# Gate and value products of two token chunks as a 2x2 block multiplication with seven products

## The chip, the cores and the metric

The kernel runs on one core of a Trainium2 chip. The metric is the time of one execution in device microseconds (us). The engines of the core are called as in the profile: PE (TensorE, matrix products), DVE (VectorE), ACT (ScalarE), POOL (GpSimd) and SP (SyncE, which issues the DMAs). Products are collected in PSUM, which has eight banks of 128 x 512 fp32; everything else lies in SBUF.

## What is computed

Attention with a mask by clusters, a first MLP with a squared ReLU, and a second MLP with a gate. The change concerns the second MLP:

```python
def _moe2_ref(x, w_gate, w_val, w_out):      # x: 1536 x 512
    gate = 1.0 / (1.0 + np.exp(-(x @ w_gate)))   # w_gate, w_val: 512 x 1536
    val = x @ w_val
    return (gate * val @ w_out).astype(np.float32)   # w_out: 1536 x 512

x = _moe_ref(x=attention, **moe_kwargs)      # relu(x @ w_in) ** 2 @ w_out
return _moe2_ref(x=x, **moe2_kwargs)
```

`w_gate` is drawn 200 times as large as the other matrices, and all is fp32.

## The kernel before

**Tiling.** The 1536 tokens are three chunks of 512 (`NCH`, numbers 0, 1, 2), the model width 512 is four tiles of 128 (`KD`), and the width 1536 of the second MLP is twelve tiles of 128 (`NF2`, index f). Tensors are kept transposed: the output y of the first MLP is, for each chunk, four tiles of 128 x 512 (feature x token), and a gate or value product of one chunk and one f is one PSUM bank of 128 x 512.

**Precision.** An fp32 factor is scaled by a power of two and split into two f16 tiles, a high part (`copy`, L368, most often on ACT) and a low part, the rest (`rest`, L1634, a SCALAR_TENSOR_TENSOR on DVE). A product of two such pairs is three matmuls: high x high, high x low, low x high. So the gate product of one (chunk, f) is 4 tiles x 3 = 12 matmuls into a bank `pg`, the value product 12 into a bank `pv` (`g3_half`); over 3 chunks and 12 f's that is 864 matmuls.

**Weights.** For each f, SP loads a raw tile `wgr` and one `wvr` (128 x 512). They are then brought to a form that can be split exactly: the magnitude on ACT (L1487), a clamp on POOL (L1495, in place), a shift and two bit operations on DVE (L1502, L1509, L1516), giving `wgm` and `wvm`. ACT takes their largest sum (L353), PE adds over partitions (bank `sm`), DVE makes the power of two (L612 to L622, tiles of 128 x 2), and the split gives the pairs `wgp` and `wvp`. The twelve `w2` tiles, for the last product, go the same way.

**A gate and value step.** When `pg` of (chunk, f) is full, ACT takes a tanh out of it (L1926, tile `th`), which frees the bank; when `pv` is full, DVE makes `gv` = (th + 1) * pv (L1933), which frees that one. ACT then bounds `gv` (L2157), PE and DVE turn the bounds of eight or four f's into powers of two (`gm`, L1769 to L1990), and `gv` is split into `gs` (ACT high, DVE low) for the last product `o`, which has 432 matmuls. U (L2138) is the small product of two powers of two that the tanh and the bound need. `yf` (L1903) adds up parts of y on DVE as their banks come.

**What sets the order.** PE's order of products is the list `order`: the first MLP of chunk 0, then of chunks 1 and 2, then the gate and value steps (`g3`), for f = 0 and 1 chunk by chunk, from f = 2 on all three chunks for each f, then `o` (`g4`). The order of every other instruction on every engine is worked out when the kernel is built, by a list scheduler (`Planner`) that has a priority and a price on each engine for each task; the table `PLAN` holds priorities and tie-breakers. An engine runs its instructions in that order, each waiting for its inputs and for its buffers: PSUM banks are handed out from pools of 1, 2, 4 and 1 banks, big tiles from a pool of slabs.

Of the kernel before, what the change touches and what calls it, by code (L numbers as in the profile page):

```python
# [33 lines left out]
    "c_hi_v": 5490, "clamp_p": -17626, "conv": 25, "conv_gate": 10, "d": -72.6, "dup_a": 10516,  # L34
    "dup_p": -33301, "dup_q": 32564, "e_bufs": 2, "exp": 0.0, "fill_less": 250, "fill_most": 12,
    "fill_step": 215, "g_gate": 121, "g_most": 14.9, "g_split": -3.9, "group": 4, "h_gate": 16,
    "h_split": -8.5, "hi": 30.7, "hi_a": -33311, "hi_p": 105282, "hip_p": 1853, "hip_v": 19873,
    "keep_x_v": -47, "kept": 1, "kept2": 0, "lead": 0, "lead2": 51, "lead_min": 9.2,
    "lead_slope": 0, "lo": -0.2, "lo_v": 18934, "load_gate": 42, "margin": 13, "max": -0.2,
    "oh_p": 86, "pe_keep": 3.3, "pe_keep_v": 15244, "pe_turn": 92.9, "pv": 2.6, "pv_pe": 65.6,  # L40
    "qk": -3.4, "qk_hi_a": -33970, "qk_hi_p": 34925, "qk_lo_v": 24610, "qk_sc_p": -14028, "raw": 27,
    "relu": -72.7, "s_hi_a": -3303, "s_hi_p": -6526, "s_lo_v": -10971, "spare": 0,
    "split_gate": 116, "square_v": 6751, "third": 1, "turn": -5.4, "v_hi_a": -4766, "v_hi_p": 15239,
    "v_later": 100000, "v_lo_v": -10993, "v_split": 4.8, "v_stat": 6.0, "w_hi_a": 4334,
    "w_hi_p": 8749, "w_lo_v": -9747, "w_load": 9.4, "w_mag_v": 20242, "w_split": 25.5,
    "wait_a": 0.19, "wait_p": 0.07, "wait_q": 0.1, "wait_t": 0, "wait_v": 0.18, "worth_a": -17439,
    "worth_p": -5542, "worth_v": 4863, "x": -1.2, "x0": 194, "x1": 67, "x_gate": 2, "x_split": 8.1,
    "y_gate": 43, "y_keep": 9.9, "y_keep_v": 30618, "y_split": 45.6,
# [162 lines left out]
def kernel(  # L211
# [13 lines left out]
    nc = tc.nc  # L225
# [384 lines left out]
    def power(src, inv, scale):  # L610
# [8 lines left out]
        nc.vector.tensor_scalar(  # L619
            out=inv, in0=inv, scalar1=float(2.0 ** -14), scalar2=None, op0=ALU.mult  # L620
        )
        nc.vector.reciprocal(out=scale, in_=inv)  # L622
# [834 lines left out]

    class Weights:
        def __init__(self, src, name, tiled, uses, whole=(), col=None, known=False):
# [4 lines left out]
            self.known = known  # L1464
            self.raw, self.m, self.parts = {}, {}, {}
            self.conv = {}
# [55 lines left out]
        def tasks(self, f, uses):  # L1522
            k = uses[0]
            pr = pr_of(k, CONV)
            t = add(
                lambda e: self.load(f), {"q": 2100}, pr - PLAN["w_load"], take=[("st", 1)],
                gate=near(k, LOADGATE),
            )

            room = (k, CONVGATE, 1)  # L1530
            t = add(
                lambda e: self.magnitude(e, f), {"a": 560, "v": 335}, pr, kind="w_mag", after=[t],
                take=[("S", 1)], gate=room,
            )
            t = add(lambda e: self.clamp(e, f), {"v": 335, "p": 600}, pr, kind="clamp", after=[t])
# [17 lines left out]
        def bound_task(self, f, k):  # L1553
            def most(e):
# [5 lines left out]
                most, {"a": 625}, pr_of(k, PLAN["w_split"]), after=[self.conv[f]], take=[("S", 1)],  # L1560
                gate=(k, SPLITGATE, 2),
            )

        def pair_tasks(self, f, k, after):
            mh = hold("S", 1, 2)
# [8 lines left out]
            def lo(e):  # L1574
# [3 lines left out]
                drop(self.m.pop(f))  # L1578

            a = add(  # L1580
                hi, {"a": 617, "v": 400, "p": 790}, pr_of(k, PLAN["w_split"]), after=after + [self.conv[f]],
                kind="w_hi", give=[mh], take=[("S", 1)] if self.known else [],
# [3 lines left out]
                lo, {"v": 664, "p": 1980}, pr_of(k, PLAN["w_split"]), after=[a], give=[mh], kind="w_lo",  # L1586
# [145 lines left out]
    xpair = {}  # L1732
    u1done = {}
# [23 lines left out]
    WG = Weights(w_gate, "wg", True, w3, col=lambda f: NF1 + 2 * f)  # L1757
    WV = Weights(w_val, "wv", True, w3, col=lambda f: NF1 + 2 * f + 1)
    wdone = {}
    for f in range(NF2):  # L1760
        wdone[f] = scale_pairs([(WG, f), (WV, f)], w3[f][0])
        for w in (WG, WV):
            w.pair_tasks(f, w3[f][0], [wdone[f]])
# [11 lines left out]
    for j, fs in enumerate(FS):  # L1775
# [9 lines left out]
        def powers(e, cs=cs, box=box):  # L1785
# [120 lines left out]
    def g3_half(e, kind, c, f, k):  # L1906
# [10 lines left out]
        if c == NCH - 1:  # L1917
            W.done(f, at_["g3", 0, f])
# [86 lines left out]

    for k, (kind, c, f) in enumerate(order):
# [39 lines left out]
        elif kind == "g2":  # L2046
# [28 lines left out]
            if tail_g:  # L2075
                k3 = at_["g3", c, 0]
# [213 lines left out]
```

## Time and profile before

| | us |
|---|---|
| median of three runs (781.5 to 783.2) | 781.68 |
| the profiled execution, its own time | 780.43 |
| its span, first to last instruction | 778.7 |
| y part of the first MLP, last stretch before the gate products | 431.7 to 494.1 |
| gate and value stage (864 matmuls `pg`, `pv`) | 494.1 to 681.5 |
| last product `o` and the end | 681.5 to 778.7 |

The profile gives each instruction's engine, line, output and inputs, start and duration. The table of stretches says how busy each engine was in each; the chain of waits follows the work that ended last back to what released it; the timeline gives one engine's instructions in order of start, where "x2" is two of a kind in a row and the second number the time from the first one's start to the last one's end. Instructions of DVE overlap a little: the next starts before the one ahead has ended, so how many fit into a stretch is read from the distance of starts, not from the durations.

### The profile page before, as it was taken

The numbers are of one execution on the slowest core, as the hardware profiler recorded it, in microseconds if no ns is written. First come the engines' busy times: TensorE is split into PE (matmuls) and PEld (weight loads), VectorE is DVE, ScalarE is ACT, GpSimd is POOL, SyncE is SP. The second block draws the span as 40 slices with busy tenths as digits, with TensorE's granted clock in tenths as the row PEclk, the third lists the DMA queues.
The fourth block names the chain that finished last, engine by engine and source line by source line (L and its number), as shares of the span: only waits on it lengthen the run. The fifth ranks groups of instructions, "written<-read, shape, count | busy, mean of one in ns | idle before, by whom it ended". The sixth has DMA issues, their size and how long they took to land.

```text
span 778.7 us, 13069 instructions
## 1 busy us (share of the span) xinstructions
PE 748.8 (96%) x4865; PEld 449.0 (58%) x4865; DVE 568.0 (73%) x1111; ACT 539.6 (69%) x1036; POOL 190.0 (24%) x240
## 2 busy tenths in 40 slices
PE   8999898799999989999999999999999999999998
PEld 5667776556565557744448888544444444444443
DVE  6899899999999998877776458964445799572012
ACT  7999899989877887699995224855555798462100
POOL 7553654444424422111222110110010021010000
PEclk9999999999999999999999999999999999999999
DMA  6767697976557787732323233322112223000012
GB/s 239 179 162 155 159 220 181 207 190 152 157 161 190 191 191 158 237 109 90 107 76 122 92 109 109 108 68 97 55 54 65 77 79 106 1 1 0 1 68 94
DMA packets 132768, 93.77 MB, mean 120 GB/s; under 512 B 114657, under 2 KB 114849, under 8 KB 132705
## 3 DMA queue, kind: packets, MB, share of 16 engines
q1 hardware_dynamic: 132704, 92.95, 43.3%
q8 instruction: 38, 0.62, 0.4%
q14 instruction: 26, 0.20, 0.1%
HBM read 60.00 MB, written 3.15 MB: 81 GB/s over the span
## 4 chain that ended last, share of the span: by engine, by line
PE 68%; DVE 14%; ACT 12%; issue 3%; DMA 2%; POOL 1%; SPq 0%; DVEq 0%; ACTq 0%
PE y L361 14%; PE pv L361 12%; PE pg L361 12%; PE o L361 12%; PE g L361 12%; DVE nm L1072 4%; ACT s L1087 3%; PE s L361 3%; ACT hl L368 3%; DVE hl L1112 3%; PE po L361 2%; DVE wo0m L1509 1%; ACT vh L368 1%; ACT e L1087 1%; DVE wo0m L1516 1%
## 5 line engine op out<-in xcount | busy, mean ns | idle before, releaser
L361 PE MATMUL pv<-y,wvp 128*128 128x512 f16 x432 | 99.3, 379 | 0.0
L361 PE MATMUL pg<-y,wgp 128*128 128x512 f16 x432 | 99.2, 379 | 0.0
L361 PE MATMUL s<-M,T 128*128 128x384 f32 x360 | 86.3, 365 | 9.7 <-DVE hl L1112 5.2
L1072 DVE TENSOR_REDUCE nm<-s 128x1 f32<-128x768 f32 x96 | 90.1, 950 | 7.3 <-PE s L361 6.7
L361 PE MATMUL o<-w2p,gs 128*128 128x512 f16 x432 | 93.5, 379 | 0.0
L361 PEld LDWEIGHTS s<-M,T 128*128 128x128 f32 x360 | 60.4, 190 | 23.2 <-DVE hl L1112 11.2
L361 PEld LDWEIGHTS <-gs 128*128 128x128 f16 x432 | 42.1, 98 | 50.6
L361 PEld LDWEIGHTS <-wgp 128*128 128x128 f16 x432 | 42.0, 98 | 50.6 <-issue 0.3
L1087 ACT ACTIVATE s<-s,nm 128x768 f32<-128x768 f32 x67 | 58.8, 877 | 16.3 <-DVE nm L1072 12.9
L361 PEld LDWEIGHTS <-wvp 128*128 128x128 f16 x432 | 41.2, 98 | 48.6
L361 PE MATMUL g<-x,wi0p 128*128 128x512 f16 x288 | 66.8, 384 | 2.0 <-DVE g_12l L1686 2.0
L1112 DVE TENSOR_TENSOR hl<-s,hl 128x768 f16<-128x768 f32 x67 | 63.6, 949 | 5.0 <-ACT hl L368 4.9
L361 PE MATMUL g<-x,wi1p 128*128 128x512 f16 x288 | 62.4, 379 | 0.0
L368 ACT ACTIVATE hl<-s 128x768 f16<-128x768 f32 x67 | 54.6, 815 | 1.1
L1966 DVE SCALAR_TENSOR_TENSOR ot<-o,G,ot 128x512 f32<-128x512 f32 x12 | 9.0, 751 | 59.6 <-PE o L361 59.6
L1933 DVE SCALAR_TENSOR_TENSOR gv<-th,pv 128x512 f32<-128x512 f32 x36 | 24.5, 683 | 38.1 <-PE pv L361 38.0
L2157 ACT ACTIVATE gs<-gv,U 128x512 f32<-128x512 f32 x36 | 25.8, 718 | 36.0 <-DVE gv L1933 36.0
L361 PEld LDWEIGHTS <-pt 128*128 128x128 f16 x1296 | 42.2, 98 | 9.4 <-issue 8.7
L361 PEld LDWEIGHTS <-wi1p 128*128 128x128 f16 x288 | 28.1, 98 | 33.8
L361 PE MATMUL po<-vh,pt 128*128 128x64 f16 x864 | 44.8, 193 | 2.5 <-DVE xp L1230 2.5
L361 PEld LDWEIGHTS <-wi0p 128*128 128x128 f16 x288 | 27.0, 99 | 34.7 <-issue 6.0
L361 PE MATMUL y<-h,wo0m 128*128 128x512 f32 x96 | 44.2, 596 | 0.8 <-DVE ptc L1185 0.8
(376 smaller groups left out, 1594.8 us busy)
## 6 DMA issues: line engine op xcount, KB each, us to landing
wi0r<-in_moe_w_in_dram SPq DMA_DIRECT2D x16, 512.0 KB, 3.9
wo0r<-in_moe_w_out_dram SPq DMA_DIRECT2D x16, 512.0 KB, 3.8
wo1r<-in_moe_w_out_dram SPq DMA_DIRECT2D x16, 512.0 KB, 3.5
wi1r<-in_moe_w_in_dram SPq DMA_DIRECT2D x12, 512.0 KB, 3.7
wgr<-in_moe_w_gate_dram SPq DMA_DIRECT2D x12, 512.0 KB, 3.3
wvr<-in_moe_w_val_dram SPq DMA_DIRECT2D x12, 512.0 KB, 4.0
w2r<-in_moe_w_out_dram SPq DMA_DIRECT2D x12, 512.0 KB, 4.2
raw<-in_q_dram SPq DMA_DIRECT2D x8, 384.0 KB, 4.1
```

The source lines that it names most:

```text
L361: nc.tensor.matmul(o, lhsT=l, rhs=r, start=a, stop=z)
L368: nc.scalar.activation(out=out, in_=in_, func=AF.Copy, scale=scale)
L1072: nc.vector.tensor_reduce(out=NM[n], in_=sc_ps[n][:, :, :HS], axis=AX.XY, op=ALU.max, negate=True)
L1087: nc.scalar.activation(out=y, in_=x, func=AF.Exp, bias=NM[n], accum_out=SM[n // NQ][:, i : i + 1],)
L1112: nc.vector.tensor_tensor(out=halves(hl[:, n % 2, 1]), in0=x[:, :, :HS], in1=halves(hl[:, n % 2, 0]), op=ALU.subtract,)
L1509: nc.vector.scalar_tensor_tensor(out=mi, in0=self.words(f)[1], scalar=-0x40000000, in1=mi, op0=ALU.bitwise_and, op1=ALU.bitwise_or,)
L1516: nc.vector.scalar_tensor_tensor(out=mi, in0=self.words(f)[0], scalar=29, in1=mi, op0=ALU.logical_shift_right, op1=ALU.bitwise_or,)
L1933: nc.vector.scalar_tensor_tensor(out=o, in0=t, scalar=1.0, in1=p, op0=ALU.add, op1=ALU.mult)
L1966: nc.vector.scalar_tensor_tensor(out=o, in0=p, scalar=by, in1=o, op0=ALU.mult, op1=ALU.add)
L2157: nc.scalar.activation(out=t.rearrange("p a k -> p (a k)").bitcast(F32), in_=gv[c, f], func=AF.Abs, scale=U3[:, c, f, 1:2], accum_out=GA[: ...
```

## The change

Chunk 0 stays as it was, 24 products of 12 matmuls. For chunks 1 and 2 two neighbouring f's are taken together: with the model width in two halves, the products of two chunks and two f's are a 2x2 matrix of blocks times another, once for the gate (`pg`) and once for the value (`pv`), so there are six pairs of f and twelve such "quads". A quad has seven block products a to g in place of eight. A block product has half the depth, 2 tiles x 3 = 6 matmuls, and a bank of its own; a quad is 42 matmuls in place of 48. What comes with it:

- Sums of weight blocks: for each pair of f's and each of `wgm`, `wvm`, four subtractions or additions of 128 x 256 into the tiles `wgs_0`, `wgs_1` (or `wvs`), 48 in all, which stand on POOL; their split gives `wgq` (or `wvq`), 24 high parts and 24 low ones.
- Sums of y blocks: eight of 128 x 512 on DVE (`yT`, L2449), after chunk 2's last `yf`, and their split. Chunks 1 and 2 now have one scale in common (`ys1`).
- A quad's results: product a is copied out of its bank by ACT (X); seven additions on DVE, each of a bank and an SBUF tile (L2224, 84 in all), join X, U, Y and Z, which become the four results.
- The tanh (L2270) and the value step (L2277) of chunks 1 and 2 then read and write SBUF tiles.
- PE's order: chunk 0 for f = 0 to 3, then in turn quad `pg` and quad `pv` of one pair and two f's of chunk 0; the last two pairs stand without chunk 0 between.
- The scale of two f's is made at once (`sm` six times with 4 columns, not twelve times with 2); the split of three `wo1` low parts stands on DVE instead of POOL. The loads are the same, in another order.

```diff
 PLAN = {
-    "c_hi_v": 5490, "clamp_p": -17626, "conv": 25, "conv_gate": 10, "d": -72.6, "dup_a": 10516,
+    "comb": 142.0, "comb_p": -23566, "comb_v": -9423, "conv": 25, "conv3": 8.1, "conv_gate": 10,
...
-    PRE = 2
-    for c in range(NCH):
-        order.extend(("g3", c, f) for f in range(PRE))
-    for f in range(PRE, NF2):
-        for c in range(NCH):
-            order.append(("g3", c, f))
+    PRE = PLAN["pre"]
+    order.extend(("g3", 0, f) for f in range(PRE))
+    for i in range(NF2 // 2):
+        order.extend((("q", "pg", i), ("q", "pv", i)))
+        order.extend(("g3", 0, f) for f in range(PRE + 2 * i, PRE + 2 * i + 2) if f < NF2)
...
+            if n == 0:
+                tt(out=x, in0=mb[:, :HD], in1=mb[:, HD:], op=ALU.add)
+                tt(out=y, in0=x, in1=ma[:, :HD], op=ALU.subtract)
+            else:
+                tt(out=x, in0=ma[:, :HD], in1=mb[:, :HD], op=ALU.subtract)
+                tt(out=y, in0=ma[:, HD:], in1=S[0][:, HD:], op=ALU.subtract)
...
+            t = add(
+                comb, {"v": 680, "p": 1400}, pr, kind="comb", after=[w.conv[a], w.conv[b]] + ([t] if t else []),
...
+        def product(nm, left, right):
+            p = Q[nm] = bank(f"{kind}{nm}{i}")
+            n = 0
+            for kk, (lh, ll) in enumerate(left):
+                rh, rl = TY[right, kk]
+                for x, y in ((lh, rh), (lh, rl), (ll, rh)):
+                    mm(p, x, y, n == 0, n == 5)
+                    n += 1
...
+                nc.vector.tensor_tensor(out=Q[out], in0=Q[one], in1=Q[other], op=ALU.add)
...
+        t = on_pe("a", lambda: cols(a, 0), "B11", prev + w1_, [wa])
...
+        t = on_pe("b", lambda: sums(1), "T2", [t] + sp[:2], [sh[0]])
+        u2 = join("U", "X", "b", t, [s1])
+        t = on_pe("c", lambda: sums(2), "T3", [t] + sp[2:], [sh[1]])
+        u3 = join("Y", "U", "c", t, [u2])
+        t = on_pe("d", lambda: sums(0), "T1", [t], [sh[0]])
+        c22 = join("Z", "Y", "d", t, [u3], free=False)
+        u4 = join("U", "U", "d", t, [c22])
+        t = on_pe("e", lambda: cols(a, 1), "B21", [t], [wa])
+        c11 = join("X", "X", "e", t, [u2])
+        t = on_pe("f", lambda: cols(b, 1), "T4", [t] + w2_, [wb])
+        c21 = join("Y", "Y", "f", t, [c22])
...
+        c12 = join("U", "U", "g", t, [u4])
...
+                o = yt[n, kk] = slab(F32, f"y{n}_{kk}")
+                eng(e).tensor_tensor(out=o, in0=src(x, kk), in1=src(y, kk), op=ALU.subtract)
```

Two engines' orders show what the planner makes of it. A row is one instruction: its line, its operation, its output tile, its inputs and its size.

DVE of the kernel before, in the middle of the gate and value stage: the low parts of one f's weights, two value steps, the conversion of the next f's weights, a value step.

```order
L1634 SCALAR_TENSOR_TENSOR wgp_2091_6777<-wgm_2079_6746,WS,wgp_2091_6777 128x512
L1634 SCALAR_TENSOR_TENSOR wvp_2093_6781<-wvm_2083_6750,WS,wvp_2093_6781 128x512
L1933 SCALAR_TENSOR_TENSOR gv_3_2108_6843<-th_3_2102_6817,pv_3_2101_6804 128x512
L1933 SCALAR_TENSOR_TENSOR gv_3_2118_6877<-th_3_2113_6860,pv_3_2112_6847 128x512
L1502 TENSOR_SCALAR wgm_2117_6875<-wgm_2117_6875 128x512
L1502 TENSOR_SCALAR wvm_2121_6879<-wvm_2121_6879 128x512
L1509 SCALAR_TENSOR_TENSOR wgm_2117_6875<-wgr_2015_6534,wgm_2117_6875 128x512
L1509 SCALAR_TENSOR_TENSOR wvm_2121_6879<-wvr_2022_6544,wvm_2121_6879 128x512
```

DVE of the changed kernel, at the second quad: a value step of chunk 0, then the seven joins of `pg`'s products b to g and the first two of `pv`'s.

```order
L2039 SCALAR_TENSOR_TENSOR gv_5_2229_7060<-th_5_2195_6976,pv_5_2190_6958 128x512
L2224 TENSOR_TENSOR pgU_2236_7074<-pgX_2201_6997,pgb_2200_6990 128x512
L2224 TENSOR_TENSOR pgY_2240_7078<-pgU_2236_7074,pgc_2204_7001 128x512
L2224 TENSOR_TENSOR pgX_2201_6997<-pgX_2201_6997,pge_2216_7032 128x512
L2224 TENSOR_TENSOR pgZ_2249_7099<-pgY_2240_7078,pgd_2209_7018 128x512
L2224 TENSOR_TENSOR pgU_2236_7074<-pgU_2236_7074,pgd_2209_7018 128x512
L2224 TENSOR_TENSOR pgY_2240_7078<-pgY_2240_7078,pgf_2223_7047 128x512
L2224 TENSOR_TENSOR pgU_2236_7074<-pgU_2236_7074,pgg_2233_7065 128x512
L2224 TENSOR_TENSOR pvU_2260_7131<-pvX_2253_7113,pvb_2250_7102 128x512
L2224 TENSOR_TENSOR pvY_2264_7141<-pvU_2260_7131,pvc_2256_7117 128x512
```

Between two pairs of weight conversions, where one value step per chunk stood, DVE now has the joins, and each of six banks of a quad is freed by one of them.

POOL of the kernel before, in the same stage: the clamps of two f's weights, and nothing between.

```order
L1495 TENSOR_SCALAR wgm_2117_6875<-wgm_2117_6875 128x512
L1495 TENSOR_SCALAR wvm_2121_6879<-wvm_2121_6879 128x512
L1495 TENSOR_SCALAR wgm_2155_7004<-wgm_2155_7004 128x512
L1495 TENSOR_SCALAR wvm_2159_7008<-wvm_2159_7008 128x512
L1495 TENSOR_SCALAR wgm_2193_7133<-wgm_2193_7133 128x512
```

POOL of the changed kernel, near the start of the stage: between the clamps stand the eight sums of one pair of f's, four for the gate (`wgs`) and four for the value (`wvs`).

```order
L1508 TENSOR_SCALAR wgm_2022_6490<-wgm_2022_6490 128x512
L1508 TENSOR_SCALAR wvm_2069_6655<-wvm_2069_6655 128x512
L1822 TENSOR_TENSOR wgs_0_2130_6796<-wgm_1934_6261 128x256
L1823 TENSOR_TENSOR wgs_0_2130_6796<-wgs_0_2130_6796,wgm_1903_6212 128x256
L1822 TENSOR_TENSOR wvs_0_2139_6814<-wvm_1978_6385 128x256
L1823 TENSOR_TENSOR wvs_0_2139_6814<-wvs_0_2139_6814,wvm_1910_6230 128x256
L1825 TENSOR_TENSOR wgs_1_2149_6835<-wgm_1903_6212,wgm_1934_6261 128x256
L1826 TENSOR_TENSOR wgs_1_2149_6835<-wgm_1903_6212,wgs_0_2130_6796 128x256
L1825 TENSOR_TENSOR wvs_1_2155_6851<-wvm_1910_6230,wvm_1978_6385 128x256
L1826 TENSOR_TENSOR wvs_1_2155_6851<-wvm_1910_6230,wvs_0_2139_6814 128x256
L1508 TENSOR_SCALAR wgm_2140_6817<-wgm_2140_6817 128x512
```

The sums stand in the queue beside the clamps of the next f's, in six such groups of eight; the first two groups stand before the last `yf` of DVE, the other four behind it.

## Rows read from the trace of the kernel before

**Rows 1.** First part of the page: busy time and share of each engine.

```profile
PE 748.8 (96%) x4865; PEld 449.0 (58%) x4865; DVE 568.0 (73%) x1111; ACT 539.6 (69%) x1036; POOL 190.0 (24%) x240
```

**Rows 2.** Table of stretches: from:to, length, busy of each engine (instructions), granted clock, DMA.

```profile
431.70:494.10 62.40, 62.40 (x278) 51.42 (x276) 40.72 (x86) 22.41 (x49) 9.55 (x14) 1.00 0.29 101
494.10:681.50 187.40, 187.40 (x882) 86.39 (x882) 124.16 (x295) 121.21 (x248) 18.25 (x24) 1.00 0.20 68
625.00:650.00 25.00, 25.00 (x118) 11.33 (x117) 24.58 (x50) 24.11 (x52) 8.04 (x8) 1.00 0.38 127
681.50:778.70 97.20, 93.41 (x435) 42.22 (x432) 27.52 (x53) 20.44 (x37) 2.73 (x4) 0.99 0.09 33
```

**Rows 3.** Chain of waits from 480 on: start, length, engine, tile, line.

```profile
494.27 2.61 PE pg L361 x12
...
678.90 2.63 PE pv L361 x12
...
702.35 72.57 PE o L361 x336
```

**Rows 4.** Timeline of DVE, 545 to 561: start, length, line, tiles.

```profile
545.36 0.75 DVE L1634 SCALAR_TENSOR_TENSOR wgp<-wgm,WS,wgp 128x512 f16<-128x512 f32 x1 [0.65 <-ACT wgp L368]
546.03 0.75 DVE L1634 SCALAR_TENSOR_TENSOR wvp<-wvm,WS,wvp 128x512 f16<-128x512 f32 x1
546.69 0.68 DVE L1933 SCALAR_TENSOR_TENSOR gv<-th,pv 128x512 f32<-128x512 f32 x1
...
552.21 0.42 DVE L1502 TENSOR_SCALAR wgm<-wgm 128x512 int32<-128x512 int32 x1
552.54 0.42 DVE L1502 TENSOR_SCALAR wvm<-wvm 128x512 int32<-128x512 int32 x1
...
553.48 0.68 DVE L1509 SCALAR_TENSOR_TENSOR wvm<-wvr,wvm 128x512 int32<-128x512 int32 x1
554.08 0.68 DVE L1516 SCALAR_TENSOR_TENSOR wgm<-wgr,wgm 128x512 int32<-128x512 int32 x1
...
559.52 0.17 DVE L615 TENSOR_SCALAR WI<-WI 128x2 int32<-128x2 int32 x1
559.73 0.17 DVE L619 TENSOR_SCALAR WI<-WI 128x2 f32<-128x2 f32 x1
...
560.01 0.28 DVE L2138 TENSOR_TENSOR U<-few,WI 128x2 f32<-128x2 f32 x3
```

**Rows 5.** Timeline of DVE, 630 to 648.

```profile
634.59 2.11 DVE L1509 SCALAR_TENSOR_TENSOR w2m<-w2r,w2m 128x512 int32<-128x512 int32 x2
...
645.18 1.10 DVE L1634 SCALAR_TENSOR_TENSOR gs<-gv,G,gs 128x512 f16<-128x512 f32 x1
646.20 0.68 DVE L1933 SCALAR_TENSOR_TENSOR gv<-th,pv 128x512 f32<-128x512 f32 x1
```

**Rows 6.** Timeline of POOL, 630 to 648.

```profile
632.01 4.14 POOL L1495 TENSOR_SCALAR w2m<-w2m 128x512 f32<-128x512 f32 x5 [0.47 <-ACT w2m L1487]
643.67 3.08 POOL L1495 TENSOR_SCALAR w2m<-w2m 128x512 f32<-128x512 f32 x2 [7.51 <-ACT w2m L1487]
```

**Rows 7.** Groups of DVE instructions, 494.1 to 681.5: count, busy us, mean ns, idle before.

```profile
L1634 DVE SCALAR_TENSOR_TENSOR gs<-gv,G,gs 128x512 f16<-128x512 f32 x29 | 21.9, 796 | 2.4 <-ACT gs L368 2.4
...
L1509 DVE SCALAR_TENSOR_TENSOR wvm<-wvr,wvm 128x512 int32<-128x512 int32 x9 | 6.1, 683 | 0.0
L1509 DVE SCALAR_TENSOR_TENSOR w2m<-w2r,w2m 128x512 int32<-128x512 int32 x8 | 6.0, 784 | 0.0
...
L1502 DVE TENSOR_SCALAR w2m<-w2m 128x512 int32<-128x512 int32 x8 | 3.8, 520 | 0.0
L1502 DVE TENSOR_SCALAR wvm<-wvm 128x512 int32<-128x512 int32 x9 | 3.8, 420 | 0.0
```

**Rows 8.** The same groups for POOL, 300 to 681.5: the block sums' nearest relative.

```profile
L1603 POOL TENSOR_TENSOR wo1l<-wo1m,wo1h 128x512 fp32r<-128x512 f32 x4 | 5.2, 1294 | 45.2 <-ACT wo1h L368 45.2
```

**Rows 9.** The same groups for ACT, 494.1 to 681.5: a high part's copy.

```profile
L368 ACT ACTIVATE gs<-gv,G 128x512 f16<-128x512 f32 x30 | 19.7, 709 | 2.5 <-DVE G L1990 2.5
```

More of the change, by code (lines that the diff above doesn't have):

```diff
@@ L1464, in __init__ @@
             self.known = known
+            self.more = more
             self.raw, self.m, self.parts = {}, {}, {}
+            self.mhold = {}
             self.conv = {}
@@ L2004, in scale_group, with unscale, w_read @@
         return [t, add(back, {"v": 140}, pr + 1, after=[t, w3done[j]])]
+    whold = {
+        (w.name, f): hold("S", 1, 3 if f % 2 == 0 else 2) for w in (WG, WV) for f in range(NF2)
+    }
+    def unscale(c, f, pr):
+        return add(
+            lambda e: nc.vector.tensor_tensor(
+                out=U3[:, c, f], in0=YI[:, c], in1=WI[:, NF1 + 2 * f : NF1 + 2 * f + 2], op=ALU.mult
+            ),
+            {"v": 125}, pr - 2, after=[ydone[c], wdone[f]],
+        )
+    def w_read(w, f):
+        if whold[w.name, f].readers == 0 and f in w.pair:
+            w.done(f, at_["g3", 0, f])
@@ new lines, in product_done, with gmost, ghi, glo @@
+    def product_done(c, f, k, t0):
+        j = int(f in FS[1])
+        k4 = at_["g4", c, (j, 0)]
+        def gmost(e):
+            t = tile_of("r", (P, CH), F32, f"gj{c}_{f}")
+            with nc.allow_low_precision(reason="only the power of two of a bound is taken from it"):
+                nc.scalar.activation(
+                    out=t, in_=gv[c, f], func=AF.Abs, scale=U3[:, c, f, 1:2],
+                    accum_out=GA[:, c, f : f + 1],
+                )
+            drop(t)
+        gbound[c, f] = add(
+            gmost, {"a": 710}, pr_of(k, PLAN["g_most"]), after=[t0], take=[("r", 1)], give=[hold("r", 1, 1)]
+        )
+        if all((c, x) in gbound for x in FS[j]):
+            gdone[c, j] = scale_group(c, j, pr_of(k, PLAN["g_most"]))
+            for x in FS[j]:
+                def ghi(e, x=x):
+                    t = xpair["g", c, x] = pair(f"gs{c}_{x}")
+                    copy(e, t[:, 0], gv[c, x], GM[:, c, x : x + 1])
+                def glo(e, x=x):
+                    y = xpair["g", c, x]
+                    gT[c, x] = [y[:, 0], y[:, 1]]
+                    rest(e, y[:, 1], gv[c, x], GM[:, c, x : x + 1], y[:, 0])
+                    drop(gv.pop((c, x)))
+                gh = hold("S", 1, 2)
+                pr4 = pr_of(k4, PLAN["g_split"] if c or j else 3) + 0.01 * x
+                a = add(
+                    ghi, HI2, pr4, after=gdone[c, j][:1], take=[("S", 1)], give=[gh], kind="s_hi",
+                    gate=near(k4, GGATE),
+                )
+                b = add(glo, LO2, pr4, after=[a], give=[gh], kind="s_lo")
+                gsplit[c, x] = [a, b]
@@ L2150 @@
             )
[L2151 to L2180 removed]
+            product_done(c, f, k, t0)
+        elif kind == "q":
+            prev = quad(c, f, k, pr, prev)
         else:
```

375 lines of the change are left out of this document (290 added, 85 removed), and 3 rows, old and new, of the table PLAN.

## The prediction
> **What bounds the kernel now.** I read the shares of the engines first: PE is busy for 96% of the span, DVE for 73%, ACT for 69%, POOL for 24% [rows 1]. The chain of waits says whether that share is the limit: it runs from one group of twelve matmuls to the next, the last gate product's chain and the last value product's as much as the first, and then through `o` in one piece [rows 3]. No other engine stands in it from the first gate product to the end of `o`. The table of stretches says the same of the stage that is changed: in 187.40 us PE is busy for 187.40, at the granted clock of 1.00, with DVE at 124.16 (66%), ACT at 121.21 (65%) and POOL at 18.25 (10%) [rows 2]. So matmuls taken out of this stage shorten it one for one, as long as the others keep up. One stretch warns: from 625 to 650 DVE was busy for 24.58 of 25.00 us, and PE still lost nothing [rows 2].
>
> **What the change removes.** The stage is 494.27 to 678.90 + 2.63 = 681.53 [rows 3], 187.26 us for 864 matmuls, 0.2167 us each. Chunk 0 keeps 24 x 12 = 288, the quads need 12 x 42 = 504, together 792. 72 fewer are 15.6 us, and PE's new stage is 171.7 us. The work of attention and of the first MLP stays, and so does `o`, whose 432 matmuls PE does nearly without a gap.
>
> **What it adds on DVE.** I count what stands in DVE's queue from the last `yf` to the last join, and price it by the distance of starts. A value step, a join or a bit operation takes 0.60 us (554.08 - 553.48), a low part 0.66 to 0.67 (546.69 - 546.03), a shift 0.33 to 0.34, a small dependent operation 0.21, a U 0.09 [rows 4]. The queue holds 84 joins and 8 block sums of y (92 x 0.602 = 55.4), 34 value steps and 48 bit operations (82 x 0.602 = 49.4), 63 low parts (x 0.664 = 41.8), 24 shifts (8.1) and 107 small ones (17.1): 171.8 us, where PE has 171.7. Joins of a bank with an SBUF tile don't occur before; the value step, which also reads a bank and an SBUF tile, is the nearest row, at 0.68 long [rows 4]. About 2 us come on top, for the y scale that DVE waits for and five dependent neighbours. So DVE goes from 66% of the stage to all of it. The 27 `gs` low parts that fall behind the last join lie in the `o` stage, where DVE was busy for 27.52 of 97.20 us [rows 2]; they cost nothing there as long as chunk 0's stand ready, and chunk 1's have until `o` of chunk 0 is through.
>
> How far may DVE be late before PE waits? PE writes eight banks, and a block product fills one in 1.30 us, so PE can be some 8 us ahead of the joins before a bank is missing. At the start it is behind by more: chunk 0's four first pairs take eight banks in 20.7 us, but the first value step stands behind 23.0 us of y sums, low parts and conversions in DVE's queue. Four of the banks are freed early, by ACT's tanh; the fifth and sixth block products need a value step's bank, and I count a wait of 1.2 us for PE there. Later the lag falls: by the ninth value step of chunk 0 DVE's sum is 1 us behind PE's, at the last join 0.3. If nothing slows DVE, 1.2 us is all that PE loses.
>
> **What it adds on POOL, and what that does to DVE.** 48 block sums of 128 x 256. An addition of 128 x 512 on POOL took 1294 ns [rows 8], half the columns then 0.65 us. Behind the last `yf` stand 32 of them and 20 clamps, 52 in place of 24. POOL itself, at 18 + 32 x 0.65 = 39 of 172 us, is no bound. But DVE's instructions are slower beside POOL's. In the dense stretch two L1509 took 2.11 us together and a `gs` low part 1.10, while POOL had five clamps in a row, then two; the value step right behind, with a bank as an input, took its 0.68 beside the same clamps [rows 5, 6]. In the groups of the stage L1509 means 784 ns for `w2m` against 683 for `wvm`, L1502 520 against 420, a `gs` low part 796 against the 750 of a quiet one [rows 4, 7]. For the eight `w2m` clamps that is (8 x 0.101 + 8 x 0.100 + 29 x 0.046) / 8 = 0.37 us of DVE for each. This is the upper end of what I take from rows; the lower is nothing, since a value step loses nothing [rows 5]. Of the 261 large instructions behind the last `yf` 96 read a bank, so I take 0.37 x 165/261 = 0.23 for each of the 52, 12.1 us, nearer to the upper end because DVE has no idle time left in which a POOL instruction could lie. DVE is then done at 171.8 + 2.0 + 12.1 = 185.9, less the 8 us by which PE may lead, 177.9: **PE loses 6.2 us**. By nothing it would be the 1.2 from above, by 0.37 for all 52 (19.2 us) it is 13.3.
>
> The Trainium skill, SBUF — State Buffer, section "Who interferes with whom", says that a DVE instruction with two SBUF inputs contends with a GpSimd instruction that reads SBUF, one with at most one SBUF input doesn't, and that the shared port is held for a whole instruction. The trace agrees in kind: 2.11 for two against 0.68 for the one with a bank [rows 5]. That rule speaks against putting the sums on POOL.
>
> **ACT and the rest.** ACT gains 12 copies of X and some 30 high parts (`wgq`, `wvq`, `yT`), less what it does anyway; at 0.71 us [rows 9] 42 x 0.71 = 30 us would bring 121.21 to at most 151 of 172. It hides under PE. In the y stage DVE was busy for 40.72 of 62.40 us [rows 2]; some 10 us of low parts and conversions move there from later or from POOL, and PE has no wait by it. SP's loads are the same. The `sm` and `ys` products change by a few tenths of a microsecond.
>
> **The sum.** 780.43 - 15.6 + 6.2 = 771.0 for the profiled execution. That execution lies 1.25 us under the median of 781.68, so I say **772.3**.
>
> **The rivals.**
> *Clean.* DVE keeps up, because POOL's sums fall beside joins and value steps that read a bank. For it: the value steps' 0.68 beside clamps. Against it: DVE's own sum already equals PE's. PE loses 0 to 3 us: 766.1 to 769.
> *DVE and POOL exclude each other.* DVE becomes the bound by more than in my sum. For it: 2.11 us for two where 1.37 is normal, and a queue with no slack. The place is the run of joins and low parts in the stage's first two thirds, where POOL's sums stand in groups of eight. Were each POOL instruction to cost DVE its full 0.65 us, 52 x 0.65 = 33.8, PE would lose 171.8 + 2.0 + 33.8 - 8 - 171.7 = 27.9 and the time be 781.68 - 15.6 + 27.9 = 794.0. It turns slower than before from a loss of 15.6 + 1.6 = 17.2 us on, which is 23.1 us of DVE or 0.44 us for each POOL instruction. Against it: 0.37 is the price in the worst stretch of the trace, and the planner sets sums apart from most of DVE's two-input work.
> *DVE's instructions don't overlap.* If a join's successor started only at its end, each of the 261 large ones would cost 0.08 us more (0.685 long at a distance of 0.602), 21 us in all, and PE would lose 171.8 + 21 + 2 - 8 - 171.7 = 15.1: 781.2, no change. Against it: the distances in the trace, 0.60 at a duration of 0.68 [rows 4], for instructions that don't depend on each other; the joins of one quad often do.
> [...]
> *Nothing is saved* can be excluded: the queue of PE holds 792 of these matmuls, not 864.
>
> **How the numbers follow.** The forecast, a loss of 3 to 11 us, 769 to 777, has 0.55; clean 0.22; exclusion, a loss over 11, 0.21, of which 0.05 lies up to 780.1, 0.06 within 0.2% of 781.68 and 0.10 above 783.2; no overlap 0.02. About 0.2% (1.6 us) is what a measurement of this kernel can tell from no change. So faster is 0.55 + 0.22 + 0.05 = 0.82, same 0.06 + 0.02 = 0.08, slower 0.10. The range goes from the clean end, 766.0, over the upper price of the rows (779.4) to 782.0, and leaves out slower and a little of the rest.
>
> **What would show it.** The gate and value stage at 172 to 180 us with DVE over 95% busy in it; gaps of PE before block products, released by joins; L2224 at about 0.68 us and 0.60 apart; low parts (L1648) longer than 0.75 where POOL works. It is clean if PE shows no gap there and DVE has idle time in the stage. It is exclusion if low parts and bit operations mean over 0.9 us. I would be wrong in kind if the gaps were released by ACT or by DMAs, if the y stage grew, or if `o` waited for `gs`.

## The result, and the profile after

| | before | changed |
|---|---|---|
| median, first comparison (4 runs each), us | 782.21 | 771.18 |
| median, second comparison (9 and 5 runs), us | 782.02 | 771.54 |
| the profiled execution, its own time, us | 780.43 | 772.25 |
| its span, us | 778.7 | 770.5 |
| y part of the first MLP, last `g` to last `y` matmul, us | 87.60 | 89.27 |
| gate and value stage, first to last matmul, us | 187.41 | 173.95 |
| `o`, from the stage's end to its last matmul, us | 93.4 | 93.5 |

The changed kernel is faster: the ratio is 0.9858 with an interval of 0.9838 to 0.9878 in the first comparison, and 0.9859 (0.9839 to 0.9878) in the second. The forecast was 772.3. So the time came out as forecast, but two of the steps that led to it did not hold, as the profile shows. The first part of the page of the changed kernel, which answers to [rows 1]:

```profile
PE 737.5 (96%) x4786; PEld 443.8 (58%) x4786; DVE 649.0 (84%) x1225; ACT 563.2 (73%) x1078; POOL 233.0 (30%) x285
```

The table of stretches of the changed kernel (columns as in [rows 2]): the y part, the gate and value stage, `o` and the end.

```profile
410.20:499.30 89.10, 87.72 (x389) 72.14 (x388) 83.58 (x141) 51.82 (x103) 39.06 (x44) 1.00 0.38 126
499.30:673.20 173.90, 172.54 (x803) 78.40 (x803) 170.88 (x366) 131.31 (x260) 38.41 (x49) 1.00 0.16 57
673.20:770.50 97.30, 93.52 (x436) 42.42 (x433) 36.67 (x73) 19.85 (x36) 0.00 (x0) 0.99 0.09 33
```

DVE is now busy for 170.88 of 173.90 us in the stage, where it had 124.16 of 187.40 [rows 2], and PE is still busy for all but 1.4. What PE waits for, from 300 us on (engine, line, released by: us in total, times, the longest):

```profile
PE sm L366 <- ACT wvp L358: 1.4, 1, 1.4
...
PE pvb L366 <- ACT pvX L373: 0.7, 1, 0.7
...
PE gm L366 <- ACT gj L2135: 0.5, 1, 0.5
```

The groups of DVE instructions in the stage, 499.3 to 673.2, that answer to [rows 7], with a join and a low part of the block sums (line numbers are those of the changed kernel):

```profile
L1522 DVE SCALAR_TENSOR_TENSOR w2m<-w2r,w2m 128x512 int32<-128x512 int32 x12 | 7.8, 693 | 0.0
...
L1648 DVE SCALAR_TENSOR_TENSOR gs<-gv,G,gs 128x512 f16<-128x512 f32 x8 | 5.9, 747 | 0.0
...
L1648 DVE SCALAR_TENSOR_TENSOR wvq<-wvs,WS,wvq 128x512 f16<-128x512 f32 x8 | 5.6, 746 | 0.0
...
L1515 DVE TENSOR_SCALAR w2m<-w2m 128x512 int32<-128x512 int32 x12 | 4.5, 427 | 0.0
...
L2224 DVE TENSOR_TENSOR pgY<-pgU,pgc 128x512 f32<-128x512 f32 x6 | 4.1, 685 | 0.2
```

The instructions that were slow beside POOL before, with means of 784, 796 and 520 ns [rows 7], are at 693, 747 and 427 now, with twice as much on POOL in the stage.

Of PE's waits the first lies in the y part, the others in the stage. By the distance of starts PE loses 1.55 us at `sm`, and in the stage 0.29 at the fourth block product, 0.84 at `pvb` and 0.25 and 0.62 at two `gm`, 2.0 us in all.

In spans, 8.2 us were gained: 13.5 in the stage, less 1.7 in the y part, 0.1 in `o` and 3.5 ahead of all that, where both kernels do the same. Thirteen profiles tell what the last is. Attention's last product (`xq`) ended at 324.6 and 325.7 us in the two profiles of the kernel before, and at 322.7 to 328.1 in the eleven of the changed kernel and its variants; this part varies from execution to execution. Stretches of one profile are therefore the better measure of what follows, and medians are good to a microsecond or two.

### The profile page after: what moved, and what is told of

The parts are those of the page before. It is cut to its first block, busy times and chain, and to the rows that moved or that the text cites. A ratio compares the mean times of both kernels' runs of the same rounds, so it can differ in the third digit from the quotient of the medians.

```text
span 770.5 us, 13165 instructions
## 1 busy us (share of the span) xinstructions
PE 737.5 (96%) x4786; PEld 443.8 (58%) x4786; DVE 649.0 (84%) x1225; ACT 563.2 (73%) x1078; POOL 233.0 (30%) x285
## 4 chain that ended last, share of the span: by engine, by line
PE 52%; DVE 27%; ACT 14%; issue 4%; DMA 2%; SPq 1%; POOL 1%; DVEq 0%; ACTq 0%
PE o L366 12%; PE g L366 12%; PE y L366 10%; DVE nm L1077 4%; PE s L366 3%; ACT s L1092 3%; ACT hl L373 3%; DVE hl L1117 3%; PE po L366 2%; DVE yf L2010 1%; PE pv L366 1%; DVE wvp L1648 1%; DVE wo0m L1522 1%; ACT vh L373 1%; DVE wvq L1648 1%
## 5 line engine op out<-in xcount | busy, mean ns | idle before, releaser
L366 PE MATMUL po<-vl,pt 128*128 128x64 f16 x432 | 42.3, 193 | 0.0
L366 PEld LDWEIGHTS <-wvp 128*128 128x128 f16 x252 | 24.4, 98 | 29.1
L366 PEld LDWEIGHTS <-wgp 128*128 128x128 f16 x252 | 24.3, 98 | 29.1 <-issue 0.3
L373 ACT ACTIVATE ot<-o,G 128x512 f32<-128x512 f32 x12 | 8.2, 685 | 42.1 <-PE o L366 41.6
L1952 ACT ACTIVATE r<-g,U 128x512 f32<-128x512 f32 x48 | 32.7, 685 | 6.5 <-PE g L366 6.4
L366 PE MATMUL pv<-y,wvp 128*128 128x512 f16 x144 | 33.1, 380 | 0.0
```

Of the source, the lines that this page charges most:

```text
L366: nc.tensor.matmul(o, lhsT=l, rhs=r, start=a, stop=z)
L373: nc.scalar.activation(out=out, in_=in_, func=AF.Copy, scale=scale)
L1952: nc.scalar.activation(out=r, in_=banks["g1", c, f], func=AF.Relu, scale=U1[:, f, c : c + 1])
```

## The experiments

Two measures are used throughout. The **stage** is the time from the first to the last gate or value matmul: 187.41 us before, 173.95 after. DVE's **excess** is worked out from the trace: for every DVE instruction the time that it took beyond its like with no POOL instruction beside it (0.685 us for 128 x 512, 0.75 for a low part, 0.42 for a shift, 0.41 for a sum of 128 x 256, 0.17 and 0.16 for small ones), summed over a stretch. Medians stand against the kernel before on the same chip.

| run | median us | ratio (95% interval) | y part | stage | excess in stage |
|---|---|---|---|---|---|
| kernel before | 781.6 to 782.2 | 1 | 87.6 | 187.4 | 4.5 |
| changed | 771.18, 771.54 | 0.9858, 0.9859 | 89.3 | 174.0 | 5.5, 4.9 |
| sums twice | 795.89 | 1.0179 (1.0150 to 1.0209) | 97.3 | 192.5 | 18.4 |
| sums on DVE | 777.41 | 0.9947 (0.9926 to 0.9968) | 88.9 | 181.8 | 3.3 |
| joins more | 788.64 | 1.0088 (1.0061 to 1.0114) | 89.3 | 185.2 | 3.4 |
| joins small | 769.05 | 0.9837 (0.9818 to 0.9856) | 89.3 | 172.8 | 3.8 |
| planner's rule off | 780.35 | 0.9983 (0.9970 to 0.9996) | 87.5 | 184.4 | 10.1 |
| extra beside joins | 780.62 | 0.9986 (0.9974 to 0.9997) | 89.3 | 181.9 | 10.4 |
| extra beside low parts | 777.94 | 0.9946 (0.9927 to 0.9965) | 89.3 | 181.9 | 11.2 |
| three products later | 769.05 | 0.9841 (0.9817 to 0.9865) | 87.5 | 174.2 | 5.5 |
| one product later | 768.22 | 0.9814 (0.9792 to 0.9835) | 87.5 | 174.1 | 5.4 |

### The two kernels once more

> The kernel before once more, for a second profile of it. In the changed kernel's profile the last product that turns attention's result (xq) ends at 328.14 us, before the first gate product of anything; in the profile of before it ended at 324.61, though both kernels do the same work there in the same order. Theory N: this part varies from execution to execution by a few us, so here it ends anywhere from 324 to 329. Theory S: the change slows this part, so here it ends at 324.6, give or take 0.5, as in the first profile. Both: time 781 to 783.

Measured: 781.6 us, ratio 1.0004 (0.9991 to 1.0018); `xq` ends at 325.74, y part and stage are 87.60 and 187.41 again.

> The changed kernel once more, on the chip of the next three. Its attention part ended at 328.14 us in the first profile; the runs since gave 324.7 to 327.5 for the changed kernel's attention and 324.6 and 325.7 for that of before. Theory N (that part only varies): here it ends anywhere from 324 to 329, the rest is as in the first profile: y part 89.3, gate and value stage 174.0. Time 770 to 772.

Measured: 771.54 us; `xq` ends at 325.98, y part 89.28, stage 173.96. Everything behind `xq` repeats to a few hundredths of a microsecond, and theory N holds: the 3.5 us of the first profile are no cost of the change.

### Is DVE the bound of the stage, or PE?

In one run the in-place joins work on 64 of their 512 columns, which leaves out most of these sums; in another the first two joins of a quad are done twice:

```diff
-                nc.vector.tensor_tensor(out=Q[out], in0=Q[one], in1=Q[other], op=ALU.add)
+                x = slice(0, CH if new else 64)
+                nc.vector.tensor_tensor(out=Q[out][:, x], in0=Q[one][:, x], in1=Q[other][:, x], op=ALU.add)
```

> The changed kernel with the 48 joins that add in place (of 84) cut to 64 of their 512 columns, so that this part of the sums is left out: about 48 x 0.5 = 24 us less DVE work in the stage. Theory A (PE is the bound of the stage already; DVE just keeps up): the stage falls from 174.0 by at most the 1.2 us of PE's waits that DVE's queue explains, to 172.8 to 174, time 770 to 771. Theory D (DVE is the bound, and matmuls are no longer what counts): the stage falls to 171.7, which is PE's work alone, and all waits of PE are gone, time 768.5 to 769.5.

```diff
-                nc.vector.tensor_tensor(out=Q[out], in0=Q[one], in1=Q[other], op=ALU.add)
+                for _ in range(2 if new and free else 1):
+                    nc.vector.tensor_tensor(out=Q[out], in0=Q[one], in1=Q[other], op=ALU.add)
```

> The changed kernel with the first two joins of each quad (U and the first Y) done twice in a row: 24 more DVE instructions of 0.60 us, 14.4 us, same result. Theory A (DVE is at its limit, with at most the 2 to 8 us by which PE may run ahead of it left): stage 182 to 190, time 779 to 787, so that the change would be lost. Theory S (DVE has room, its 170.9 busy us of 173.9 overstate it): stage under 178, time under 775.

The stage in the tables of stretches, with the short joins and then with the doubled ones, there with `o` behind it:

```profile
497.30:670.10 172.80, 171.95 (x803) 78.59 (x803) 151.58 (x369) 131.70 (x263) 38.99 (x49) 1.00 0.16 58
```

```profile
496.30:681.50 185.20, 176.23 (x803) 79.50 (x803) 180.32 (x381) 131.17 (x260) 39.12 (x49) 0.98 0.15 54
681.50:785.90 104.40, 96.01 (x435) 43.18 (x433) 41.89 (x81) 19.85 (x36) 0.00 (x0) 0.96 0.08 31
```

With 19 us less DVE work the stage is 1.2 us shorter, and the two waits at `gm`, 0.9 us together, are gone. That is theory A, at the lower end of its range for the stage; the waits at the first quad stay, so it is not D's 171.7. The median, 769.05, would fit theory D, but lies under A's bound by no more than attention varies. With 14.4 us more DVE work the stage is 11.2 us longer, and `o` is 7.1 us longer, so the kernel is slower than before. The stage is in theory A's range; the time lies 1.6 us above it, because of `o`, and PE's waits with the doubled joins tell why:

```profile
PE gm L366 <- ACT gj L2135: 11.3, 4, 4.2
PE sm L366 <- ACT wvp L358: 2.0, 2, 1.4
PE pvd L366 <- DVE pvU L2225: 0.9, 1, 0.9
```

PE stands at `gm`, not at a bank. `gm` adds up the bounds of eight or four f's; it needs DVE's last value step among them and ACT's bound of it, and it stands in PE's queue soon behind those products. So it ties PE to DVE more closely than eight banks do. The waits have a second price. From the timeline of PE in this run, about the wait ahead of the first `gm`:

```profile
582.78 1.03 PE L366 MATMUL pge<-y,wgp 128*128 128x512 f16 x4
586.55 0.37 PE L366 MATMUL gm<-GA,every 128*128 128x8 f32 x1 [2.75 <-ACT gj L2135]
...
587.00 2.74 PE L366 MATMUL pgf<-yT,wgp 128*128 128x512 f16 x6
589.54 1.62 PE L366 MATMUL pgg<-y,wgq 128*128 128x512 f16 x6
```

From the start of `pgf`, soon behind the wait, to that of the next product it is 2.54 us; a block product of the changed kernel takes 1.29. The granted clock there is 0.50, PE's lower level of 1.2 GHz. Both runs together place the changed kernel near the knee: DVE costs PE about 1 us in the stage, and what 14.4 us more of DVE work cost is more than these 14.4. No run adds only a microsecond or two, so where exactly the loss sets in is not shown.

### What do POOL's sums cost DVE?

> The changed kernel with every block sum of the weights done twice in a row on POOL (96 in place of 48, same result). Theory A, from the trace of the changed kernel: POOL's sums cost DVE almost nothing, since the planner set them beside joins, and where they meet DVE's two-input work POOL is the one that waits (one clamp took 5.86 us). Then the time is within 1.5 us of the changed kernel's 771.2, and the gate and value stage stays at 174 to 175.5 us. Theory P, the term of my sum: each POOL instruction costs DVE 0.23 us and DVE is at its limit, so 32 more cost 7.4 us: stage 179 to 182, time 777 to 779.

The sums were put into a loop of two. Measured: 795.89, stage 192.5, y part 97.3. Theory A fell, and P's price was too low. The excess rose by 13 us in the stage, 0.4 us for each of 32 more sums, and PE's waits came on top. Of the 18.4 us of excess 13.6 stand on small instructions. The stage, and a stretch of it behind a wait of 2.75 us at an `sm`:

```profile
506.60:699.10 192.50, 179.41 (x803) 80.19 (x803) 184.84 (x366) 131.59 (x260) 65.60 (x81) 0.96 0.14 52
...
574.00:577.40 3.40, 3.40 (x9) 1.14 (x8) 3.27 (x6) 3.40 (x7) 3.08 (x6) 0.51 0.39 151
```

The granted clock of that stretch is 0.51, PE's lower level of 1.2 GHz, soon after it had stood still; in the changed kernel's stage it is 1.00 throughout.

> The changed kernel with the 48 block sums of the weights on DVE in place of POOL, at the same place in the program. A sum of 128x256 should take DVE 0.3 to 0.35 us, 48 of them 15 us, 32 of these behind the last yf: 10 us more for a DVE that was busy for 170.9 of 173.9 us. Theory A (DVE is at its limit in this stage, POOL's sums cost it little): PE loses most of these 10 us, less the 2 to 6 us by which DVE is early enough: stage 178 to 184, time 776 to 781. Theory P (each POOL instruction costs DVE 0.23 us, so taking them away gives 7.4 us back): stage 174 to 177, time 771 to 774.

```diff
-            tt = eng(e).tensor_tensor
+            tt = nc.vector.tensor_tensor
```

Measured: 777.41, stage 181.8, as theory A has it. A sum took DVE 0.41 to 0.43 us with no POOL instruction beside it, not the 0.30 to 0.35 expected. DVE's excess falls only to 3.3 us, 1.6 of it on sums beside POOL's clamps, so 28 sums fewer on POOL give back about 2 us where their own time costs DVE 11. POOL is the right place for them.

So why were 48 sums cheap, and 48 more dear? The trace of the changed kernel has an answer. DVE beside the sums of one pair of f's, and POOL at the same time:

```profile
533.70 0.68 DVE L2224 TENSOR_TENSOR pgY<-pgU,pgc 128x512 f32<-128x512 f32 x1
534.30 0.68 DVE L2224 TENSOR_TENSOR pgX<-pgX,pge 128x512 f32<-128x512 f32 x1
534.89 0.68 DVE L2224 TENSOR_TENSOR pgZ<-pgY,pgd 128x512 f32<-128x512 f32 x1
```

```profile
533.22 0.73 POOL L1822 TENSOR_TENSOR wvs<-wvm 128x256 f32<-128x256 f32 x1
534.04 0.73 POOL L1823 TENSOR_TENSOR wvs<-wvs,wvm 128x256 f32<-128x256 f32 x1
534.73 0.72 POOL L1825 TENSOR_TENSOR wgs<-wgm,wgm 128x256 f32<-128x256 f32 x1
```

Neither hinders the other. Over the whole stage 28 sums lie on POOL, for 21.4 us; for 16.8 of these DVE is at an instruction that reads a bank, and for 1.1 at a large one with two SBUF inputs. And where POOL meets a run of DVE's low parts, it can be POOL that waits. DVE and POOL once more, a little earlier:

```profile
514.20 4.06 DVE L1648 SCALAR_TENSOR_TENSOR yT<-yT,few,yT 128x512 f16<-128x512 f32 x6
518.18 1.41 DVE L1648 SCALAR_TENSOR_TENSOR wgq<-wgs,WS,wgq 128x512 f16<-128x512 f32 x2
519.51 1.41 DVE L1648 SCALAR_TENSOR_TENSOR wvq<-wvs,WS,wvq 128x512 f16<-128x512 f32 x2
```

```profile
518.17 5.86 POOL L1508 TENSOR_SCALAR wvm<-wvm 128x512 f32<-128x512 f32 x1 [15.16 <-ACT wvm L1500]
```

The clamp that takes 0.61 us alone was held for 5.86, and the low parts beside it took their usual time. What does suffer is small. DVE's scale of two f's behind a run of joins, while POOL has its clamps:

```profile
563.69 0.65 DVE L617 TENSOR_SCALAR WI<-WS 128x2 f32<-128x2 f32 x1
564.38 0.54 DVE L620 TENSOR_SCALAR WI<-WI 128x2 int32<-128x2 int32 x1
564.95 0.17 DVE L624 TENSOR_SCALAR WI<-WI 128x2 f32<-128x2 f32 x1
```

```profile
563.71 1.18 POOL L1508 TENSOR_SCALAR w2m<-w2m 128x512 f32<-128x512 f32 x2
```

0.65 and 0.54 in place of 0.17: of the 4.9 to 5.5 us of excess in the stage, 4.8 are small instructions. Some 3.4 us of it stand on TENSOR_SCALARs with one SBUF input of two or eight columns, the rest on small ones with two SBUF inputs, the U's above all. The Trainium skill, SBUF — State Buffer, section "Who interferes with whom", says that a `tensor_scalar` can take the pair of ports that DVE shares with GpSimd when it runs in a two-port mode, an exception that the prediction had left out; the trace agrees that this form waits for POOL, even at two columns, but doesn't show in which mode it ran.

Two runs then put the same POOL work beside joins, and beside low parts. It writes into a tile (`ident`) that nothing reads any more:

```diff
+                if out == "Z":
+                    for x in range(4):
+                        nc.gpsimd.tensor_tensor(out=ident, in0=Q[out][:, x * P : (x + 1) * P], in1=ident, op=ALU.add)
```

> The changed kernel with 48 idle additions of 128x128 more on POOL, four behind each quad's join Z, whose result they read: they start when Z is made and run beside the joins U, Y and U that follow on DVE, each of which reads a bank. Theory A (what counts is what DVE does at the time: joins don't suffer beside POOL): DVE's excess in the stage, 4.9 us in the changed kernel, rises by less than 2 us, the stage stays at 174 to 175.5, time 770.5 to 773. Theory P (each POOL instruction costs DVE a part of its length, wherever it lies, some 0.1 to 0.15 us for one of this size): excess up by 5 to 7 us, stage 177 to 181.

```diff
             rest(e, t[:, 1], S[n], sc, t[:, 0])
+            if i >= 2:
+                for x in range(4 - 2 * n):
+                    nc.gpsimd.tensor_tensor(out=ident, in0=t[:, 1, x * P : (x + 1) * P], in1=ident, op=ALU.add)
```

> The same number of idle additions on POOL, 48 of 128x128, but behind the low parts of the block sums (four behind each first low part, two behind each second, for the pairs of f from 4 on): they start when a low part is made and run beside the next low parts or conversions, which have two SBUF inputs. Theory A: DVE's excess in the stage rises by 5 us or more, PE waits longer by most of that, stage 177 to 182, time 774 to 780. Theory B (POOL waits for DVE, not DVE for POOL, as with the clamp that took 5.86 us beside eight low parts): excess up by less than 2 us, stage 174 to 175.5, time 770.5 to 773.

Measured: excess 10.4 and 11.2 us, stage 181.9 in both, medians 780.62 and 777.94. Beside low parts theory A's numbers came, beside joins nearly those of P (the stage is 0.9 us longer than it said). In both the stage grew by 7.9 us, for 5.5 and 6.3 us more of excess. The joins themselves were not hindered. POOL and DVE of the first of the two runs:

```profile
560.51 2.06 POOL L2227 TENSOR_TENSOR ident<-pgZ,ident 128x128 f32<-128x128 f32 x4 [0.36 <-DVE pgZ L2224]
...
566.88 2.89 POOL L2227 TENSOR_TENSOR ident<-pvZ,ident 128x128 f32<-128x128 f32 x4 [0.97 <-DVE pvZ L2224]
569.74 1.05 POOL L1508 TENSOR_SCALAR wvm<-wvm 128x512 f32<-128x512 f32 x1
```

```profile
560.95 0.68 DVE L2224 TENSOR_TENSOR pgY<-pgY,pgf 128x512 f32<-128x512 f32 x1
561.54 0.68 DVE L2224 TENSOR_TENSOR pgU<-pgU,pgg 128x512 f32<-128x512 f32 x1
...
567.85 1.60 DVE L1648 SCALAR_TENSOR_TENSOR wgq<-wgs,WS,wgq 128x512 f16<-128x512 f32 x2
569.37 1.96 DVE L1648 SCALAR_TENSOR_TENSOR wvq<-wvs,WS,wvq 128x512 f16<-128x512 f32 x2
```

The four additions behind `pgZ` run beside joins of 0.68. Those behind `pvZ`, and the clamps that now come later on POOL, meet the low parts that follow on `pv`'s joins, and two of these take 1.96 us where two take 1.41. In this run the additions lay for 13.6 us beside DVE instructions that read a bank, but for 10.0 us beside large ones with two SBUF inputs, and the clamps' time beside such rose from 5.8 to 13.0 us. So beside joins POOL's work cost DVE nothing here too; in both runs the cost came where the added work, or what it pushed later, met other instructions, 0.11 and 0.13 us for each small addition. Beside low parts POOL waited at 518 us of the changed kernel, and here DVE does; what decides which of them waits, no run shows.

> The changed kernel, but the planner may set the block sums of the weights anywhere on POOL: for these 24 tasks its rule is taken away that a task of POOL and a task of DVE with two SBUF inputs don't run at the same time (DVE's order changes at some places with it). In the changed kernel DVE's instructions of the y part took 12.1 to 12.5 us more than alone, beside 43 POOL instructions, 0.29 us for each; those of the gate and value stage 4.9 to 5.5 us beside 48, 0.11 for each, since there the sums lie beside joins, which read a bank. Theory A (it is this placing that makes the sums cheap in the stage): more of them meet conversions and low parts, DVE's excess in the stage rises to 8 us or more, stage 176 to 182, time 773 to 780. Theory B (joins and POOL's own waiting make them cheap wherever they stand): stage 174 to 175, time 770 to 772.

```diff
-                gate=(k, PLAN["split_gate3"], 3),
+                gate=(k, PLAN["split_gate3"], 3), port="",
```

Measured: 780.35, excess 10.1, stage 184.4: A's numbers, but not a clean test. In this order the planner also set eight low parts between two joins of the first gate quad (535.3 to 541.0 us), and a wait of PE of 3.9 us at the last product of the first value quad is due to them; of the low parts there only one was slowed, to 1.09. The excess doubled with the rule taken away, and the sums did change their place: for 5.6 of their 25.3 us they lay beside instructions that read a bank, where it had been 16.8 of 21.4. How much of the 10.5 us of stage is due to that, and how much to the order, this run doesn't tell.

### The wait in the y part, and a faster version

The chain of waits of the changed kernel, at the end of the y part:

```profile
495.58 0.61 DVE wgm L1529
496.22 0.62 ACT wgp L358
496.88 0.73 ACT wvp L358 x2
497.93 1.51 PE y L366 x6
```

PE stands amid the last `y` bank for `sm`, the sum of the weight bounds of f = 4 and 5, which the quads need some 50 us later. DVE converts those weights late, since it is busy for 83.58 of 89.10 us in this part, with an excess of 12.1 to 12.5 us beside 43 POOL instructions, 0.29 us each (before: 1.6 us, 19 instructions). There are no joins there to lie beside. How much of the lateness is this excess, and how much the work that the change moved there, no run separates.

```diff
-            mm(box[0][:, :4], every, AB[:, c0 : c0 + 4], True, True)
+            f = lambda: mm(box[0][:, :4], every, AB[:, c0 : c0 + 4], True, True)
+            plan.next.append(f) if i == 2 else f()
```

`plan.next` holds a product back until PE's next task is written. With this and all `gm` one task later:

> The changed kernel with three kinds of small products set one step later in PE's order: the sum over partitions of the weight bounds of f = 4 and 5 (sm, at 495.9 us) stands behind the last y products instead of amid them, and each gm product one block product later. In the changed kernel's trace PE waited 1.55 us at that sm for an ACT bound that it needs only some 50 us later, and 0.25 and 0.62 us at two gm. Theory A: these waits are lost for good, because PE is the bound; without them the kernel is 2.0 to 2.6 us faster, 768.6 to 769.4. Theory D: DVE is the bound behind them, so that the time that PE gains here it waits at the next bank: under 0.8 us faster, 770.4 to 771.4.

Measured: 769.05; y part 87.49, stage 174.19, `o` 94.28. The time is theory A's, but by luck: in the three stretches only 0.8 us were gained, and the rest of the 2.5 us between the medians is within what attention varies. Only the `sm` gave anything, 1.78 us; the waits at `gm` moved with `gm` (1.0 us in two pieces), and those of `o` cost 0.77. So only the `sm` was moved:

> The changed kernel with one small product moved: sm of f = 4 and 5 stands behind the last y products instead of amid them; the gm products stay where they are. Theory A, from the run with all three moves (its y part was 1.78 us shorter, its gate and value stage the same, its o part 0.77 longer because of the gm products moved there): y part 87.5, stage 174, o 93.5, so 1.8 us faster than the changed kernel run beside it. Theory D (what PE gains there it waits again at the first quad, since DVE's queue is as long): stage 175 to 176, under 0.5 us faster.

The table of stretches of this version, y part, stage, `o` and end:

```profile
404.80:492.10 87.30, 87.30 (x387) 72.03 (x385) 83.06 (x141) 51.10 (x101) 37.69 (x42) 1.00 0.36 122
492.10:666.20 174.10, 172.54 (x803) 78.39 (x803) 171.06 (x365) 132.16 (x264) 41.32 (x51) 1.00 0.17 61
666.20:763.80 97.60, 93.83 (x437) 42.60 (x435) 36.97 (x73) 19.86 (x36) 0.00 (x0) 1.00 0.09 33
```

Measured: 768.22 us, ratio 0.9814 (0.9792 to 0.9835), beside 771.54 for the changed kernel on the same chip. By stretches 1.8 us are gained in the y part and 0.2 lost in the stage, as theory A says; the rest of the 3.3 us between the medians is within what attention varies. Of the versions that compute the same result this one is the fastest, by the sum of the three stretches too.

## Why the prediction was right, and where it was not

**The matmuls.** 72 fewer at 0.2167 us, 15.6 us: right. With its waits of 2.0 us taken from 173.95, 171.9 are left of PE's stage, where 171.7 were counted.

**DVE's own sum.** 171.8 us and the two that come on top, against PE's 171.7: right in kind and nearly in size. The last join ended 175.5 us after the last `yf`, with some 5 us of excess in it, so DVE's own sum was a few microseconds too high. Joins are 0.68 us long and 0.60 apart, the distance of the value step, which was the row that stood for them. The rival without overlap fell with that. The lag fell nearly as counted: the first value step of chunk 0 started 18.8 us behind its product, the ninth 2.9, the last join 1.7, where 1 and 0.3 had been counted for the last two. PE's wait at the first quad, put at 1.2 us, was 1.1, but only 0.29 of it was a wait for a value step's bank, the one that was counted. The other 0.84 stood at `pvb`, which got a bank from ACT's copy of `pva` at 531.5 us, while DVE's first join began at 532.4.

**POOL's price for DVE: the step that failed.** A sum of 128 x 256 takes POOL 0.73 us, not 0.65, but that is no matter. I put 12.1 us on DVE for 52 POOL instructions at 0.23 each. In the stage stood 48, since 28 sums fell into it and not 32, and the excess was 4.9 to 5.5 us, 0.11 each; and 4.5 us of such excess had stood in that stage before, so the change added 1 us at most. I had thinned out the price by the share of joins among DVE's instructions, as if sums fell on them by chance. By that share 7.9 of the sums' 21.4 us would lie beside instructions that read a bank; the planner's order put 16.8 there. Doubling the sums shows that POOL does cost DVE time when its work doesn't fit, at 0.4 us each more than my upper price, though two thirds of that rise fell on small instructions and not on those that I had priced. Low parts and bit operations did not suffer in the changed kernel's stage; small ones did, which I had not looked at. (Two L1509 in a row without POOL take 1.28 us, not the 1.37 that I set beside the 2.11; no step of the sum hangs on it.)

**The 8 us by which PE may lead.** Also wrong, with the other sign. DVE's 12 us were to be cut to 6 by it, but the doubled joins show that PE waits at `gm` long before it runs out of banks. Had the 12.1 us come, PE would by that run have lost most of them: there 14.4 us more cost 18.3 with `o`. The two errors lay against each other.

**The y part.** "PE has no wait by it" failed: 1.7 us. There the price of 0.23 for a POOL instruction would have been about right (0.29), and I had not applied it.

**The sum.** PE's loss against its own work is 2.3 us in the stage and 1.7 in the y part, 4.0, where 6.2 was forecast for the stage alone. Of the rivals it was the clean one that held in the stage (0 to 3 us). That the time came within 1.1 us of the forecast is luck: a price for POOL that was too high in the stage was made up in part by a wait elsewhere that had been put at nothing. With that wait moved, the run of one product later came at 768.22, within the clean rival's 766.1 to 769. Two of the signs that I had named for being wrong in kind did appear: the y part grew, and of PE's waits only the 0.29 us was released by DVE, the others by ACT. At `sm` and `gm` ACT itself had waited for DVE, so DVE's lateness stands behind these, by a way that the prediction did not have. The remaining difference between 772.3 and 771.2 to 771.5 is less than attention varies.

**ACT** went to 131 of 174 us, under the bound of 151, and `o` did not wait for `gs`: right.

## What to carry to other kernels

When work is taken off the bound engine and put on another, add up the other's queue over that stage at its distances of starts: here it came out equal to the bound; joins cut short gave back 1.2 us, and 14.4 us more cost over 18, so the change had next to nothing to spare. Price contention by place, not by mean: ask which DVE instructions stand beside each POOL instruction, and in which part of the kernel nothing that reads a bank is there to shield it. And look in the queue of the bound engine for small products that need a late result early (`sm`, `gm`); one of these, moved by six matmuls, was worth more than any other wait that these runs took away.

## What the runs showed of the hardware

- A POOL instruction can be held for many DVE instructions in a row: a clamp of 0.61 us took 5.86 beside a run of low parts, which were not slowed. With more on POOL low parts were slowed, two of them to 1.96 us from 1.41.
- DVE's TENSOR_SCALAR on 128 x 2, 0.17 us alone, took up to 0.65 beside POOL in the stage, and 1.16 at the worst (L620 at 475.05 us in the y part). In the changed kernel's stage small instructions, most of them of this kind, made up nearly all of DVE's excess.
- Joins of 512 columns with one bank and one SBUF input took 0.67 to 0.70 us beside POOL's additions as without them, in every run.
- After PE had stood still for 2.75 us, in two runs, a block product ran at the lower clock (granted 0.51 and 0.50, 1.2 GHz), and it was 2.53 and 2.54 us from its start to the next one's, against 1.29 at 1.00 (2.4 GHz). Such a wait can cost more than itself. It need not: behind waits of 3.00 us (at `pgd`, sums twice) and 3.48 us (at `gm`, extra beside joins) the granted clock stayed at 1.00.
